# The end of an attention stage reordered: the cap load, two third-chunk sums, the second batch's normalization, and the decoding of one weight unit

## The chip, the core and the metric

The kernel runs on one core of one Trainium2 chip. The metric is the device time of one execution in microseconds (us), lower being better. Engines are called by the profile's names: PE (TensorE matmul) and PEld (TensorE weight load), DVE (VectorE), ACT (ScalarE), POOL (GpSimd), SP (SyncE, which issues most transfers).

## What is computed

Attention with a soft cap over 2 batches, 12 heads, 448 tokens and 64 columns a head, then two feed-forward blocks on the 896 tokens. Cut to what matters here:

```python
scores = cap * tanh((q @ k.T) / sqrt(64) / cap)
attn = softmax(scores)                       # per row
x = (attn @ v) for all heads, as [896 tokens, 768]
h = x @ w_in;  x = (h * sigmoid(1.702 * h)) @ w_out            # d_ff 2048
xn = x / rms(x) * rms_g
out = (silu(xn @ w_gate) * (xn @ w_val)) @ w_out2              # d_ff 1536
```

All inputs and outputs are float32.

## The kernel before, in words

**Attention** (`attention`, lines 174 to 508) works on 12 pairs of heads, p = 0 to 11; pairs 0 to 5 are batch 0, pairs 6 to 11 batch 1. One loop (line 435) runs p from 0 to 12, the last round being only a tail. The order of instructions on every engine is the order of the calls, written by hand. In one round ACT takes tanh and exp of pair p's scores (lines 292 and 295; the first tanh of pair 0 is line 262), TensorE makes the outputs of pair p - 1 (line 314) and the scores of pair p + 1 (line 246), and DVE casts the next q and k (lines 223, 224), copies out pair p - 1 (line 327) and finishes an earlier pair. The scores of each pair come in three chunks of 128 keys and a fourth of 64 keys. `tsc`, the factor of every tanh, is worked out on DVE from the cap (lines 216, 217).

The row sums of exp are made in steps. `add_two` (line 333, DVE) adds chunks one and two into a tile `ts`. `add_third` (line 335) has two meanings: for pair 11 DVE adds the third chunk (line 337); for pairs 1 to 9 (`LAST`, line 329) POOL issues two accumulating transfers that add the fourth chunk. `sums(p)` (line 345) lets TensorE sum over keys by products with ones: one stream for `ts`, one for the third chunk unless it is already in `ts`, and one with `blk` for the fourth chunk unless it is. Each stream is four matmuls, which show as 8 records of line 356. DVE then transposes, takes the reciprocal and transposes again (lines 361, 363, 365). `spread` (line 369) distributes the result by four transfers, for pair 11 two of them from ACT's queue.

`norm(p)` is three steps: `norm_mul` (line 378, DVE) multiplies the output by the reciprocal sums, `norm_hi` writes a rounded copy (line 383 on DVE, line 385 on ACT for pairs 10 and 11), `norm_lo` (line 390, DVE) writes what the rounding left. Both parts go to the feed-forward input x. Round 10 normalizes pairs 4 and 5, round 11 pairs 6 and 7, the tail pairs 8 to 11.

**Feed-forward** (`rest`, from line 510) is a stream of TensorE columns. A column is one block of 128 outputs for one side of the tokens (b = 0: tokens 0 to 383, b = 1: tokens 384 to 895), 18 matmuls (lines 566 to 568, high weight with high x, high weight with low x, low weight with high x, six times). The first ten columns take, as (weight unit i, side b), (0,0), (1,0), (0,1), (1,1), (2,1), (3,1), (2,0), (3,0), (4,0), (5,0). They are called columns 0 to 9 here. b = 1 needs all pairs of batch 1.

**Weights** arrive as 64-bit words and each unit is decoded in six steps: `scale` (line 129, ACT), `shift` (133), `top` (137), `low` (143), all on DVE and all in one tile `dec`; then `high_part` (line 155, ACT) writes the high weights into the ring, and `low_part` (line 160, DVE) the low ones. `low(w)` for w > 2 also starts the load of unit w + 3; units 0 and 1 are decoded in the attention rounds. Unit 2's `scale` runs in round 12 on ACT, its `shift` between the steps of pair 10's normalization, its `top` ahead of pair 11's `norm_mul`, its `low` between pair 11's `norm_hi` and `norm_lo`.

Work that follows a column is put into a list by `at` and carried out in order by `tick` (line 527). Behind column 0 the list is: the rest of pair 11's normalization, then `gate` (line 592, ACT, which needs a new activation table), `high` (line 595, ACT) and `rest_` (line 598, DVE), which waits for `high`; then the list `first` (line 622): scale 3; shift, top, low, high_part, low_part of unit 2 as far as not done; shift, top, low of 3; scale 4; high_part 3, scale 5, shift 4, top 4; then `load_to(5)`. Behind column 1 follow low 4, `rest_` of column 1, and low_part 3.

Of the kernel before, what the change touches and what calls it, by code (L numbers as in the profile page):

```python
# [17 lines left out]
def attn_moe_kernel(  # L18
# [14 lines left out]
    nc = tc.nc  # L33
# [10 lines left out]
    NPR = B * NP  # L44
# [4 lines left out]
    def f(ap):  # L49
        return ap.bitcast(F32)  # L50

    keep = ctx.enter_context(tc.tile_pool(name="keep", bufs=1))
    capt = keep.tile([128, 1], F32, name="capt")
# [108 lines left out]
    def run(op, w):  # L162
        if w < len(units) and (op, w) not in done:
            done.add((op, w))
            op(w)
# [8 lines left out]
    def attention():  # L174
        with ExitStack() as actx:
# [15 lines left out]
            xs, raws, vs, pa, pb, zt, nr, ts_ = {}, {}, {}, {}, {}, {}, {}, {}  # L191
# [15 lines left out]
            cuts = [slice(0, S), slice(64, 192), slice(192, XW - S), slice(0, 64)]  # L207
# [121 lines left out]
            LAST = range(1, NPR - 2)  # L329
# [3 lines left out]
                nc.vector.tensor_tensor(out=ts_[p], in0=pa[p][:, 0], in1=pa[p][:, 1], op=ALU.add)  # L333

            def add_third(p):
                if p == NPR - 1:
                    nc.vector.tensor_tensor(out=ts_[p], in0=ts_[p], in1=pb[p][:, 0:2], op=ALU.add)
                elif p in LAST:
                    for j in range(2):
                        nc.gpsimd.dma_start(  # L340
                            out=ts_[p][half[j], :, j * SH:(j + 1) * SH],
                            in_=pb[p][half[j], 2].rearrange("p (e s) -> p e s", e=2), accum_op=ALU.add,
                        )

            def sums(p):
                ps = ps_s.tile([128, 2, 512], F32, tag="s", name="s")[:, 0]
                streams = [ts_[p], *([] if p == NPR - 1 else [pb[p][:, 0:2]]), *([] if p in LAST else [None])]
                for n, some in enumerate(streams):
                    for e in range(2):
                        for j in range(2):  # L350
                            if some is None:
                                w, t = blk[:, 64 * j:64 * j + 32], pb[p][:, 2, e * SH:(e + 1) * SH]
                            else:
                                w, t = f(ones)[:, 0:32], some[:, e, j * SH:(j + 1) * SH]
                            r0 = 64 * j + 32 * e
                            nc.tensor.matmul(  # L356
                                out=ps[r0:r0 + 32, 0:SH], lhsT=w, rhs=t,
                                start=(n == 0), stop=(n == len(streams) - 1), skip_group_check=True,
                            )
                by_token = zrp.tile([128, SH // 32, 32], F32, tag="bt", name="bt", bufs=2)  # L360
                nc.vector.transpose(out=by_token.rearrange("p b t -> p (b t)"), in_=ps[:, 0:SH])
                few = zrp.tile([128, SH // 32], F32, tag="few", name="few", bufs=2)
                nc.vector.reciprocal(out=few, in_=by_token[:, :, 0])
                nr[p] = zrp.tile([128, SH], F32, tag="rs", name="rs", bufs=2)
                nc.vector.transpose(  # L365
                    out=nr[p], in_=few.rearrange("p (b o) -> p b o", o=1).to_broadcast([128, SH // 32, 32]),
                )
# [9 lines left out]
            def norm_mul(p):  # L377
                nc.vector.tensor_tensor(out=zt[p], in0=zt[p], in1=nr.pop(p), op=ALU.mult)

            def norm_hi(p):  # L380
                b, pp = divmod(p, NP)
                if p < NPR - 2:
                    nc.vector.tensor_copy(xA[0][:, pp, b * S:(b + 1) * S], zt[p])
                else:
                    nc.scalar.activation(out=xA[0][:, pp, b * S:(b + 1) * S], in_=zt[p], func=AF.Copy)

            def norm_lo(p):
                b, pp = divmod(p, NP)
                xx = slice(b * S, (b + 1) * S)
                nc.vector.tensor_tensor(  # L390
                    out=xA[1][:, pp, xx], in0=zt.pop(p), in1=f(xA[0][:, pp, xx]), op=ALU.subtract
                )

            def norm(p):
                for step in (norm_mul, norm_hi, norm_lo):
                    step(p)

            nc.vector.memset(f(xA[0][:, 0, 0:S]), 1.0)
            ts = first_kq()
            nc.scalar.dma_start(out=ts[0], in_=q[0])  # L400
            nc.scalar.dma_start(out=ts[2], in_=k[0, :, cuts[2]])
            nc.scalar.activation(out=tiny, in_=f(ones)[:, 0:1], func=AF.Tanh)
            nc.sync.dma_start(out=ts[1], in_=k[0, :, cuts[1]])
            nc.sync.dma_start(out=capt, in_=cap.rearrange("(o n) -> o n", o=1).to_broadcast([128, 1]))
            nc.sync.dma_start(out=ts[3], in_=k[0, :, cuts[3]])
            constants()
            load_kq(1)
# [22 lines left out]
            scale_by_cap()  # L430

            RAW = {1: 1, 3: 2, 4: 3, 10: 4}
            NORMS = {10: (4, 5), 11: (6, 7), 12: ()}

            for p in range(NPR + 1):
                load_kq(p + 3 if p < 2 else p + 4)
                load_v(p + 2)
                if p == 1:
                    load_kq(5)
                if p in RAW:  # L440
                    load_to(RAW[p])
                if p == 0:
                    first_scores()
                    scores(0, 1)
                    tanh(0, 1)
                    exp(pa[0][:, 0])
                    scores(0, 2)
                    tanh(0, 2)
                    scores_last(0)
                    tanh(0, NC)  # L450
                    exp(pa[0][:, 1])
                    exp(pb[0])
                    outputs(0, (0,))
                    split_kq(1)
                    for c in range(NC):
                        scores(1, c)
                    outputs(0, (1,))
                elif p < NPR:
                    for c in range(NC):
                        tanh(p, c)  # L460
                subtract = cast_kq(p + 2) if p + 2 < NPR else None
                for n in NORMS.get(p, (p - 6,) if p >= 6 else ()):
                    norm(n)
                decode(p, "b")
                if subtract:
                    subtract()
                decode(p, "c")
                if p >= 1:
                    if p == NPR:
                        add_third(p - 1)  # L470
                        sums(p - 2)
                        spread(p - 2)
                    if p < NPR:
                        outputs(p - 1, (NC,))
                        scores_last(p)
                        outputs(p - 1, range(NC) if p > 1 else (2,))
                    else:
                        outputs(p - 1)
                    if p < NPR:
                        copy_out(p - 1, "D")  # L480
                    done_ = p - 1 if p == 1 or p == NPR else p - 2
                    if done_ not in nr:
                        if p == NPR:
                            norm(8)
                        sums(done_)
                        if p == NPR:
                            copy_out(p - 1, "A")
                        spread(done_)
                        if p == NPR:
                            norm(9)  # L490
                if 1 <= p < NPR:
                    tanh(p, NC)
                    exp(pa[p])
                    exp(pb[p])
                if p < NPR:
                    add_two(p)
                    decode(p, "d")
                    if p < NPR - 1:
                        add_third(p)
                if p >= 1:  # L500
                    for c in range(NC):
                        scores(p + 1, c)
            norm_mul(NPR - 2)
            norm_hi(NPR - 2)
            run(shift, 2)
            norm_lo(NPR - 2)
            q_ = NPR - 1
            return lambda: norm_mul(q_), lambda: norm_hi(q_), lambda: run(low, 2), lambda: norm_lo(q_)

    def rest(*norm_last):  # L510
        with ExitStack() as fctx:
# [70 lines left out]
            def later(*fns):  # L582
                at(1, *[("D", True, fn) for fn in fns])
# [27 lines left out]
            for c in range(NC1):  # L611
# [15 lines left out]
                for n, (i, b) in enumerate(order):  # L627
                    last = ()
                    if c == 0 and n == 0:
                        later(lambda: run(top, 2), *norm_last)  # L630
                        last = (
                            lambda: [run(*some) for some in first], lambda: load_to(5), load_g,
                        )
                    ffn1(gA, u0 + i, i, b, slots[n], last)
# [245 lines left out]
```

## Time and profile before

| | us |
|---|---|
| three runs, median | 581.82 |
| three runs, lowest and highest | 581.73, 582.35 |
| the profiled execution, its own time | 581.33 |
| its span, first to last instruction | 579.5 |

| engine | busy us | share of the span |
|---|---|---|
| PE | 573.1 | 99% |
| PEld | 493.4 | 85% |
| DVE | 411.7 | 71% |
| ACT | 274.0 | 47% |
| POOL | 59.1 | 10% |

Times inside the profile count from the span's first instruction. Instructions that follow each other on one engine overlap by their pipelines, so the distance from start to start can be a little under a duration. A releaser named behind an idle time is inferred: it is what ended last before the waiting instruction began.

### The profile page before, as it was taken

What the parts mean: (1) busy time and instruction counts of PE and PEld (TensorE: products, weight loads), DVE (VectorE), ACT (ScalarE), POOL (GpSimd) and SP (SyncE); (2) the same over time, 40 slices, a digit from 0 to 9 for tenths busy, and PEclk for the clock granted to TensorE, in tenths of its full rate; (3) what the DMA queues carried; (4) which work ended last, traced back from release to release, by engine and by line L of the source; (5) the groups of instructions that cost most, each with busy time, mean ns of one, the idle gap of its engine ahead of it and who ended that gap; (6) DMA issues with size and microseconds to landing.
All of it is one profiled execution on the core that took longest, in us unless ns stands there. A gap on an engine that the chain in (4) does not pass through costs nothing.

```text
span 579.5 us, 9374 instructions
## 1 busy us (share of the span) xinstructions
PE 573.1 (99%) x3842; PEld 493.4 (85%) x3842; DVE 411.7 (71%) x568; ACT 274.0 (47%) x369; POOL 59.1 (10%) x54
## 2 busy tenths in 40 slices
PE   8999999999999999999999999999999999999997
PEld 5566668988899998999998989889898998989887
DVE  3889997956653365656787999873787894778732
ACT  7999965755241355553444543442243431334300
POOL 0223300000000000000313013000222000222000
PEclk9999999999999999999999999999999999999999
DMA  8898643642624123233141514351232361232022
GB/s 282 243 225 219 113 116 91 200 146 92 198 67 152 55 81 127 96 123 118 56 156 63 165 59 160 109 164 54 58 110 106 110 217 55 63 108 102 1 92 100
DMA packets 60363, 70.31 MB, mean 121 GB/s; under 512 B 4128, under 2 KB 56480, under 8 KB 60320
## 3 DMA queue, kind: packets, MB, share of 16 engines
q1 hardware_dynamic: 57136, 66.91, 35.5%
q0 software_dynamic: 2592, 2.07, 3.0%
q10 hardware_dynamic: 592, 0.74, 0.4%
q8 instruction: 30, 0.49, 0.3%
q14 instruction: 13, 0.11, 0.1%
HBM read 62.13 MB, written 2.75 MB: 112 GB/s over the span
## 4 chain that ended last, share of the span: by engine, by line
PE 95%; ACT 3%; DMA 1%; issue 0%; DVE 0%; SPq 0%; ACTq 0%
PE b L568 28%; PE b L567 28%; PE b L566 28%; PE v L314 5%; PE s L246 3%; PE s L356 2%; ACT pa L292 1%; PE s L273 1%; ACT pb L292 1%; ACT pb L295 1%; DMA capt<-in_cap 1%; ACT pa L295 1%; ACT pa L262 0%; PE b L705 0%; DVE oacc L775 0%
## 5 line engine op out<-in xcount | busy, mean ns | idle before, releaser
L568 PE MATMUL b<-x,ring 128*128 128x384 f32 (+1 forms) x480 | 174.0, 363 | 0.0
L567 PE MATMUL b<-x,ring 128*128 128x384 f32 (+1 forms) x480 | 173.8, 362 | 0.0
L566 PE MATMUL b<-x,ring 128*128 128x384 f32 (+1 forms) x480 | 173.7, 362 | 0.0
L566 PEld LDWEIGHTS b<-x,ring 128*128 128x128 f32 x480 | 90.1, 188 | 9.8 <-DVE rs L365 0.4
L568 PEld LDWEIGHTS b<-x,ring 128*128 128x128 f32 x480 | 90.1, 188 | 9.6 <-DVE ring L160 0.3
L567 PEld LDWEIGHTS b<-x,ring 128*128 128x128 f32 x480 | 90.1, 188 | 9.6
L160 DVE TENSOR_TENSOR ring<-dec,ring 128x768 fp32r<-128x768 f32 x68 | 77.2, 1136 | 28.1 <-ACT ring L155 28.1
L568 PE MATMUL b<-g,ring 128*128 128x512 f32 (+1 forms) x192 | 69.7, 363 | 0.0
L567 PE MATMUL b<-g,ring 128*128 128x512 f32 (+1 forms) x192 | 69.6, 363 | 0.0
L566 PE MATMUL b<-g,ring 128*128 128x512 f32 (+1 forms) x192 | 69.5, 362 | 0.0
L155 ACT ACTIVATE ring<-dec 128x768 fp32r<-128x768 f32 x66 | 55.2, 837 | 29.8 <-DVE dec L143 24.5
L143 DVE SCALAR_TENSOR_TENSOR dec<-raw,dec 128x768 uint32<-128x768 uint32 x68 | 66.8, 983 | 1.2
L137 DVE SCALAR_TENSOR_TENSOR dec<-raw,dec 128x768 uint32<-128x768 uint32 x68 | 64.8, 953 | 1.0
L129 ACT ACTIVATE dec<-raw 128x768 f32<-128x768 f32 x66 | 59.8, 907 | 5.2 <-issue 2.5
L568 PE MATMUL b<-uA,ring 128*128 128x512 f32 (+1 forms) x144 | 52.1, 362 | 0.0
L567 PE MATMUL b<-uA,ring 128*128 128x512 f32 (+1 forms) x144 | 52.1, 362 | 0.0
L566 PE MATMUL b<-uA,ring 128*128 128x512 f32 (+1 forms) x144 | 52.1, 362 | 0.0
L737 POOL TENSOR_TENSOR a<-a,gg 128x512 f32<-128x512 f32 (+1 forms) x18 | 29.2, 1621 | 187.1 <-DVE gg L730 160.1
L598 DVE TENSOR_TENSOR g<-gg,g 128x384 fp32r<-128x384 f32 (+1 forms) x32 | 20.0, 624 | 39.7 <-ACT g L595 39.7
L740 ACT ACTIVATE uA<-a 128x512 fp32r<-128x512 f32 (+1 forms) x24 | 13.9, 580 | 70.3 <-POOL a L737 52.0
L133 DVE TENSOR_SCALAR dec<-dec 128x768 uint32<-128x768 uint32 x68 | 39.5, 581 | 0.0
L567 PEld LDWEIGHTS b<-g,ring 128*128 128x128 f32 x192 | 36.0, 188 | 3.9
(89 smaller groups left out, 665.5 us busy)
## 6 DMA issues: line engine op xcount, KB each, us to landing
raw<-in_moe_w_out SPq DMA_DIRECT2D x20, 768.0 KB, 4.2
raw<-in_moe_w_in SPq DMA_DIRECT2D x16, 768.0 KB, 4.5
raw<-in_moe_w_gate SPq DMA_DIRECT2D x12, 768.0 KB, 4.2
raw<-in_moe_w_val SPq DMA_DIRECT2D x12, 768.0 KB, 4.3
raw<-in_moe_w_out SPq DMA_DIRECT2D x8, 512.0 KB, 3.6
v<-in_v SPq DMA_DIRECT2D x11, 256.0 KB, 5.1
r<-rs SPq DMA_DIRECT2D x46, 56.0 KB, 3.1
kq<-in_k SPq DMA_DIRECT2D x11, 224.0 KB, 4.9
```

The source lines that it names most:

```text
L129: nc.scalar.activation(out=f(d), in_=f(hi), func=AF.Copy, scale=2.0 ** -112)
L133: nc.vector.tensor_scalar(out=d, in0=d, scalar1=3, scalar2=None, op0=ALU.logical_shift_left)
L137: nc.vector.scalar_tensor_tensor(out=d, in0=hi, scalar=0x80000000, in1=d, op0=ALU.bitwise_and, op1=ALU.bitwise_or)
L143: nc.vector.scalar_tensor_tensor(out=d, in0=lo, scalar=29, in1=d, op0=ALU.logical_shift_right, op1=ALU.bitwise_or)
L155: nc.scalar.activation(out=t[:, 0], in_=f(dec_t[w][0]), func=AF.Copy)
L160: nc.vector.tensor_tensor(out=t[:, 1], in0=f(d), in1=f(t[:, 0]), op=ALU.subtract)
L314: nc.tensor.matmul(out=ps[32 * n:32 * n + 32, j, 0:SH], lhsT=w[:, d0:d0 + 32], rhs=t, start=not before, stop=len(before) == NC, skip_group ...
L566: nc.tensor.matmul(out=wide(o, b), lhsT=w0, rhs=x0, start=first, stop=False)
L567: nc.tensor.matmul(out=wide(o, b), lhsT=w0, rhs=x1, start=False, stop=False)
L568: nc.tensor.matmul(out=wide(o, b), lhsT=w1, rhs=x0, start=False, stop=last)
L598: nc.vector.tensor_tensor(out=gA[1].at(i, hb), in0=gg[0], in1=f(gA[0].at(i, hb)), op=ALU.subtract)
L737: eng.tensor_tensor(out=t[0], in0=t[0], in1=t[1], op=ALU.mult)
```

## The change

Four things are changed.

1. The cap is loaded first on SP's queue, ahead of the first chunk of k; the second piece of that pair's k (`ts[2]`, on ACT's queue) keeps its place in its queue.
2. For pairs 9 and 10 DVE adds the third chunk into `ts`, as for pair 11, so `sums(9)` and `sums(10)` have one stream less. Pair 9 keeps its accumulating transfers, now behind that addition.
3. Round 10 normalizes only pair 4, round 11 only pair 5. Pairs 6 and 7 are normalized in the tail around `sums(11)`; behind them come the steps of pairs 8, 9 and 10, interleaved, with `norm_hi` of 8 and 9 on ACT too; then pair 11.
4. `shift`, `top` and `low` of unit 2 are no longer called between those steps. They run from the list `first`, so behind column 0's `rest_`.

```diff
-                if p == NPR - 1:
+                if p >= NPR - 3:
                     nc.vector.tensor_tensor(out=ts_[p], in0=ts_[p], in1=pb[p][:, 0:2], op=ALU.add)
-                elif p in LAST:
+                if p in LAST:
...
-                streams = [ts_[p], *([] if p == NPR - 1 else [pb[p][:, 0:2]]), *([] if p in LAST else [None])]
+                streams = [ts_[p], *([] if p >= NPR - 3 else [pb[p][:, 0:2]]), *([] if p in LAST else [None])]
...
-                if p < NPR - 2:
+                if p < NPR - 4:
                     nc.vector.tensor_copy(xA[0][:, pp, b * S:(b + 1) * S], zt[p])
...
             nc.scalar.dma_start(out=ts[0], in_=q[0])
+            nc.sync.dma_start(out=capt, in_=cap.rearrange("(o n) -> o n", o=1).to_broadcast([128, 1]))
+            nc.sync.dma_start(out=ts[1], in_=k[0, :, cuts[1]])
             nc.scalar.dma_start(out=ts[2], in_=k[0, :, cuts[2]])
             nc.scalar.activation(out=tiny, in_=f(ones)[:, 0:1], func=AF.Tanh)
-            nc.sync.dma_start(out=ts[1], in_=k[0, :, cuts[1]])
-            nc.sync.dma_start(out=capt, in_=cap.rearrange("(o n) -> o n", o=1).to_broadcast([128, 1]))
...
-            NORMS = {10: (4, 5), 11: (6, 7), 12: ()}
+            NORMS = {10: (4,), 11: (5,), 12: ()}
...
                         if p == NPR:
-                            norm(8)
+                            norm(6)
                         sums(done_)
                         if p == NPR:
                             copy_out(p - 1, "A")
                         spread(done_)
                         if p == NPR:
-                            norm(9)
+                            norm(7)
+                            for step, n in (
+                                (norm_mul, 8), (norm_hi, 8), (norm_mul, 9), (norm_hi, 9), (norm_lo, 8),
+                                (norm_mul, 10), (norm_hi, 10), (norm_lo, 9), (norm_lo, 10),
+                            ):
+                                step(n)
...
-            norm_mul(NPR - 2)
-            norm_hi(NPR - 2)
-            run(shift, 2)
-            norm_lo(NPR - 2)
             q_ = NPR - 1
-            return lambda: norm_mul(q_), lambda: norm_hi(q_), lambda: run(low, 2), lambda: norm_lo(q_)
+            return lambda: norm_mul(q_), lambda: norm_hi(q_), lambda: norm_lo(q_)
...
-                        later(lambda: run(top, 2), *norm_last)
+                        later(*norm_last)
```

## Rows read from the trace of the kernel before

**Rows 1.** The page, busy time, share of the span and instructions of each engine.

```profile
PE 573.1 (99%) x3842; PEld 493.4 (85%) x3842; DVE 411.7 (71%) x568; ACT 274.0 (47%) x369; POOL 59.1 (10%) x54
```

**Rows 2.** The chain that ended last, in order of time: start us, us, what.

```profile
0.76 0.38 SPq L403
1.19 3.89 DMA capt<-in_cap
5.56 1.16 ACT pa L262 x2
...
78.33 1.89 PE s L356 x40
```

**Rows 3.** Windows: stretch, length, busy time of each engine, granted clock, DMA share, GB/s.

```profile
140.00:300.00 160.00, 160.00 (x799) 144.17 (x799) 95.01 (x123) 69.60 (x107) 5.96 (x5) 1.00 0.34 109
```

**Rows 4.** Timeline of PE: start us, us, engine, line, operation, tiles, shapes, count.

```profile
78.53 0.56 PE L356 MATMUL s<-pb,ones 128*32 128x224 f32 x8
...
98.41 0.39 PE L566 MATMUL b<-x,ring 128*128 128x512 f32 x1
...
102.71 0.39 PE L567 MATMUL b<-x,ring 128*128 128x512 f32 x1
103.00 0.50 PE L568 MATMUL b<-x,ring 128*128 128x512 f32 x1
```

**Rows 5.** Waits from 98 to 110 us: who waited for whom, total, times, longest.

```profile
PEld b L568 <- DVE ring L160: 0.3, 1, 0.3
```

**Rows 6.** Timeline of DVE, from the tail to unit 3.

```profile
81.33 1.09 DVE L337 TENSOR_TENSOR ts<-ts,pb 128x896 f32<-128x896 f32 x1
...
87.55 0.62 DVE L378 TENSOR_TENSOR z<-z,r 128x448 f32<-128x448 f32 x1
88.08 0.55 DVE L133 TENSOR_SCALAR dec<-dec 128x768 uint32<-128x768 uint32 x1
88.81 0.63 DVE L390 TENSOR_TENSOR x<-z,x 128x448 fp32r<-128x448 f32 x1 [0.18 <-ACT x L385]
89.36 0.95 DVE L137 SCALAR_TENSOR_TENSOR dec<-raw,dec 128x768 uint32<-128x768 uint32 x1
90.22 0.62 DVE L378 TENSOR_TENSOR z<-z,r 128x448 f32<-128x448 f32 x1
...
93.91 0.56 DVE L598 TENSOR_TENSOR g<-gg,g 128x384 fp32r<-128x384 f32 x1 [1.67 <-ACT g L595]
95.45 0.96 DVE L160 TENSOR_TENSOR ring<-dec,ring 128x768 fp32r<-128x768 f32 x1 [0.97 <-ACT ring L155]
96.32 0.55 DVE L133 TENSOR_SCALAR dec<-dec 128x768 uint32<-128x768 uint32 x1
...
97.90 0.96 DVE L143 SCALAR_TENSOR_TENSOR dec<-raw,dec 128x768 uint32<-128x768 uint32 x1
...
102.00 0.95 DVE L160 TENSOR_TENSOR ring<-dec,ring 128x768 fp32r<-128x768 f32 x1
```

**Rows 7.** Timeline of ACT, behind column 0.

```profile
91.54 1.28 ACT L592 ACT_TABLE_LOAD   x1
...
94.58 0.83 ACT L155 ACTIVATE ring<-dec 128x768 fp32r<-128x768 f32 x1
```

**Rows 8.** DMA issues from 91 to 98.5 us: count, size, us from issue to landing.

```profile
raw<-in_moe_w_in SPq DMA_DIRECT2D x1, 768.0 KB, 4.5
```

**Rows 9.** Timeline of PE at the start: first scores of pair 0.

```profile
4.08 1.12 PE L256 MATMUL s<-first,first 64*128 64x224 f32 x4
...
5.74 0.95 PE L246 MATMUL s<-first,first 64*128 64x448 f32 x4
```

**Rows 10.** DMA issues of the first 6 us, the first chunk of k on SP's queue.

```profile
first<-in_k SPq DMA_DIRECT2D x1, 64.0 KB, 2.6
```

**Rows 11.** Timeline of PE at the start: the last two warm-up products.

```profile
3.20 0.95 PE L417 MATMUL s<-x,ones 128*128 128x448 f32 x2
3.57 0.58 PE L417 MATMUL s<-x,ones 128*128 128x448 f32 x1
```

## The prediction, made before the changed kernel ran

> **What bounds the kernel now.** First the busy times: TensorE works for 99% of the span [rows 1], so only what shortens its work, or makes it wait, can move the time much. Next the chain of waits: it begins with the cap's transfer (1.19 to 5.08 us) and ScalarE's first tanh at 5.56, and late in the attention it lies on TensorE's sums [rows 2]. Then the stretches of the feed-forward part: between 140 and 300 us TensorE is busy in all 160.00 us [rows 3]. There is no gap later that could swallow a delay: a microsecond lost at 100 us is lost at the end. Last the timelines around the hand-over. In TensorE's there is one hitch: in column 5 the first product with unit 3's low weights starts at 103.00, 0.29 after the product before it [rows 4], where 19 products from 98.41 to 102.71 lie 0.226 apart. The waits name the cause: VectorE's low_part [rows 5], which ran from 102.00 to 102.95 [rows 6]. So before the change unit 3's decoding on VectorE is already just in time, with nothing in hand. That is what the reader should keep in view.
>
> **Part 1, shorter sums.** Two third-chunk streams go, of 8 records each; the next eight records start 0.38 later (78.53 to 78.91, as the stream of pair 10 does), so TensorE is done 0.76 sooner [rows 4]. VectorE pays two additions of 1.09 [rows 6], in rounds 9 and 10. The cover is that rounds 10 and 11 each lose one normalization, at least two instructions of 0.6; without that cover TensorE's outputs would wait for the copy-out behind them. Pair 9's two POOL transfers now wait for VectorE's addition; behind them on POOL's queue is nothing of the attention, and their sum is read only at 78 us, some 8 us later. Cost nothing.
>
> **Part 2, the tail of the normalization.** From the addition for pair 11 to pair 11's multiplication (81.33 to 90.22 [rows 6]) the list on VectorE changes as follows. Gone are shift 2 (88.08 to 88.81, 0.73 with a wait of 0.18) and top 2 (89.36 to 90.22, 0.86): 1.59. New are four steps, two multiplications and two subtractions, at 0.53 from start to start (87.55 to 88.08): 2.12. The rounded copies of pairs 8 and 10 are made on ScalarE with a subtraction waiting behind each: I put 0.18 for each, as in the row at 88.81: 0.36. The start of all this is earlier by up to 0.38, because sums(9) ends that much sooner and VectorE was waiting on it; I take 0.38. Sum: 2.12 + 0.36 - 1.59 - 0.38 = 0.51 later. Bounds: 0 if the copies are quite hidden and a step is shorter, 1.2 if nothing is gained at the start and each wait doubles.
>
> Pair 11's multiplication then starts at 90.73. For pair 10 the subtraction ended 1.89 after the multiplication's start (87.55 to 88.81 + 0.63), so pair 11's low half is there at 92.62. TensorE wants it in column 2's seventeenth product, 20 products ahead of 98.41: at 93.89 before, at 93.13 with the shorter sums. Half a microsecond in hand: no wait there. Pairs 6 to 10 are earlier still, and the reciprocals of pair 11, spread by ACT's and SP's queues, leave no later than before. All six outputs and reciprocals of the batch now live together, but the normalizations of pairs 4, 5 and 6 free each buffer ahead of its next use.
>
> **Part 3, unit 2's decoding, which decides.** Before, VectorE's wait for ScalarE (rounded copy of pair 11, table load of 1.28 [rows 7], gate, high) was partly filled with low 2, and shift and top had gone before. Now all three stand behind `rest_`, which waits for ScalarE. From pair 11's multiplication to `rest_` it was 93.91 - 90.22 = 3.69, all of it paced by ScalarE, which has no less to do; so `rest_` comes 0.51 later, at 94.42. From `rest_` to low_part 2 it was 95.45 - 93.91 = 1.54 [rows 6]. Now it is 0.47 for `rest_` (0.56, less the 0.09 by which VectorE's instructions overlap at 95.45 and 96.32), 1.58 for shift and top (96.32 to 97.90, unit 3's), 0.96 for low, 0.04 to ScalarE, 0.83 for high_part [rows 7], 0.04 back: 3.92. That is 2.38 more, or 2.89 with part 2. So low_part 2 starts at 98.34, and ends at 99.30.
>
> TensorE would be in column 4 at 98.41 - 0.76 = 97.65. It waits there some 0.65 for the high weights and 0.55 for the low ones. From low_part 2 to low_part 3 VectorE takes 6.55 (95.45 to 102.00 [rows 6]) in one unbroken string that includes column 1's `rest_`; so low_part 3 runs from 104.89, and the product that started at 103.00 starts at 105.89, after a wait of about 2.4. From there both engines are late by the same 2.89, and TensorE never catches up [rows 3]. The 0.76 of part 1 is eaten by these waits.
>
> One queue hangs on this: unit 5's load on SP waits for low 2, which ended near 91.7 (90.22 + 0.53 + 0.96) and now ends at 97.43. It lands 4.5 later [rows 8], at 101.9; ScalarE takes it behind unit 3's high_part, at 97.90 + 0.96 + 0.04 + 0.83 + 2.89 = 102.62. It is covered by 0.7; beyond that each microsecond of delay would be paid in full, since column 1's `rest_` and low_part 3 stand behind it.
>
> **Part 4, the cap first.** The tanh factor was ready at 5.5. The first scores (four records) start at 4.08 and end at 5.20; those of the next chunk end at 5.74 + 0.95 = 6.69 [rows 9], and ScalarE, done with two tanh at 6.72 [rows 2], takes them at once. So an earlier cap lets the first two tanh begin, but the third must still wait for TensorE: a gain of 0.05 at most. Against it, the first k chunk is issued 0.43 later (1.19 for 0.76). It landed at 0.76 + 2.6 = 3.36 [rows 10], and its use at 4.08 leaves 0.72. If it takes over the cap's 3.89 with its place [rows 2], it lands at 5.08 and all is 1.0 later. With 2.6 from 1.19 it lands at 3.79. The second is the nearer row, since it is the same transfer; some delay behind the cap's 128 small packets is likely, and I put a loss of 0.10. By the Trainium skill, DMA: Bandwidth & Descriptors, Queues, rings and completion order, a transfer's completion is reported only after the same engine's earlier writes; that would tie the chunk to the end of the cap's writes and speaks for the larger loss, 585.7 in all. No row shows the chunk behind the cap.
>
> **Sum.** 2.89 + 0.10 = 2.99 on the profiled execution's 581.33 (span 579.5): 584.3. That execution lies 0.49 under the median of 581.82, so the forecast is **584.8**. The case's own ends are 2.38 - 0.05 (part 2 at 0) and 3.58 + 1.00 above the median: 584.2 to 586.4.
>
> **Rivals.** (a) The decoding is not the bound and TensorE keeps part 1: faster. The place is unit 3's low_part: it would have to start near 101.0 instead of 104.89, that is, the three steps of unit 2 must find room ahead of `rest_`. Then 0.76, the hitch of 0.06 and 0.05 for the cap are saved: 580.9. For it: VectorE idles 1.67 there. Against it: VectorE takes its list in order, and the list puts them behind.
>
> (b) TensorE's clock falls in the waits. The last warm-up products, 448 columns, start 0.37 apart [rows 11], 0.83 ns a column, where 512 columns later take 0.226, 0.44 ns: two speeds a factor of two apart, though the granted clock's row says 1.00 of the later stretch [rows 3]. If the wait of 2.4 costs the higher level for one column's 18 products, that is 18 x 512 x 0.39 ns = 3.6 more: 588.4. Against it: the waits are broken up by products. The Trainium skill, TensorE: Matmul & The Clock Gate, Part 1, has idle time put the engine to 1.2 GHz and work bring back 2.4; by that rule a wait this long may or may not do it, and no row of this trace has a wait of the kind.
>
> (c) The delay is absorbed: 581.8, if TensorE had waits later on that shrink. The stretch from 140 to 300 has none.
>
> **Chances.** Forecast 0.84; (a) 0.07; (b) 0.06; (c) 0.03. A change under 0.2% (1.2 us) can't be told from none. Faster 0.07, same 0.03, slower 0.90. The range takes the case's own ends with a little below, where the copies and the start of the tail are better than put: 583.9 to 586.4. It leaves out (a), (b) and (c), 0.16 in all.
>
> **What would show it.** On VectorE after the change: shift, top and low of unit 2 behind the first L598, low_part 2 near 98.3 and low_part 3 near 104.9. On TensorE: waits for the ring in columns 4 and 5, about 1.2 and 2.4, and all later columns 2.9 late. The sums of pairs 9 and 10 with one stream less, column 0 some 0.7 sooner. The first tanh before 5.56 but the third not before 6.7. I am wrong if columns 4 and 5 start without a wait, or if TensorE waits in column 2 for pair 11, or if unit 5's load, not VectorE, ends the wait.

## The result, and the profile after

| | before | changed |
|---|---|---|
| median, us | 581.73 | 588.07 |
| lowest and highest of five, us | 580.99, 582.35 | 586.34, 588.12 |
| span of the profiled execution, us | 579.5 | 584.6 |

The changed kernel is slower: ratio 1.0104, 95% interval 1.0091 to 1.0117. The forecast of 584.8, with a range up to 586.4, had the sign and the main place of the loss, but only 3.0 of the 6.3 us. The profiled execution took 586.34; it is the fastest of the five. The other four had spans of 586.0 to 586.3 and a mean granted clock of 0.997 where this one has 1.000, and that difference is one of the two things that had to be found out. One run of a later kernel, the profiled one of the cap alone, took 818.52 at a granted clock of 0.658; it is left out, so that experiment has times but no profile to read.

The page's busy times, against [rows 1]: TensorE has 16 instructions less, as meant, but is busy for a smaller share.

```profile
PE 574.5 (98%) x3826; PEld 493.6 (84%) x3826; DVE 413.6 (71%) x568; ACT 275.1 (47%) x371; POOL 59.0 (10%) x54
```

The chain that ended last (start us, us, what), against [rows 2]. It began with the cap's transfer; now it begins with the first piece of k, and with TensorE's first scores.

```profile
1.19 3.96 DMA first<-in_k
5.29 1.86 PE s L256 x8
7.15 1.51 PE s L246 x4
...
97.63 0.97 DVE dec L137
98.62 0.97 DVE dec L143
99.62 0.85 ACT ring L155
100.49 0.96 DVE ring L160
```

Its lower half is the decoding of unit 2, none of which was on the chain before. The transfers of the first 6 us (size, us from issue to landing), against [rows 10] and these further rows of the kernel before:

```profile
first<-in_q ACTq DMA_DIRECT2D x1, 224.0 KB, 2.9
first<-in_k ACTq DMA_DIRECT2D x1, 128.0 KB, 4.3
...
first<-in_k SPq DMA_DIRECT2D x1, 32.0 KB, 4.0
```

In the changed kernel:

```profile
first<-in_q ACTq DMA_DIRECT2D x1, 224.0 KB, 4.2
...
first<-in_k SPq DMA_DIRECT2D x1, 64.0 KB, 4.0
...
capt<-in_cap SPq DMA_DIRECT2D x1, 0.5 KB, 3.7
```

The cap was issued 0.44 sooner and was used at 4.44 in place of 5.11. But q, on the other queue and issued at the same time (0.75), took 4.2, and the piece of k, now second, 4.0 in place of 2.6. TensorE and ScalarE at the start, against [rows 9] and these two rows of the kernel before:

```profile
5.74 1.70 PE L246 MATMUL s<-first,first 64*128 64x448 f32 x8
```

```profile
6.73 1.01 ACT L292 ACTIVATE pa<-s,tsc 128x896 f32<-128x896 f32 x1
```

In the changed kernel:

```profile
5.29 1.86 PE L256 MATMUL s<-first,first 64*128 64x224 f32 x8 [1.13 <-DMA first<-in_k]
6.91 3.22 PE L246 MATMUL s<-first,first 64*128 64x448 f32 x8
```

```profile
6.44 1.38 ACT L262 ACTIVATE pa<-s,tsc 128x448 f32<-128x448 f32 x2 [3.26 <-PE s L256]
8.68 1.01 ACT L292 ACTIVATE pa<-s,tsc 128x896 f32<-128x896 f32 x1 [0.86 <-PE s L246]
```

The third tanh, at 6.73 before, starts at 8.68: 1.95 later. Of this 1.21 is the wait for the transfers (4.08 to 5.29), and 0.74 lies between the first scores and the third tanh, 3.39 in place of 2.65: the eight products of line 246 span 3.22 in place of the 1.70 that they took before.

VectorE at the hand-over, against [rows 6]; 1.95 is to be taken off each time to compare. Between the second and the third row lie shift, top and low of unit 2, from 97.04 on.

```profile
92.88 0.62 DVE L378 TENSOR_TENSOR z<-z,r 128x448 f32<-128x448 f32 x1
...
96.57 0.56 DVE L599 TENSOR_TENSOR g<-gg,g 128x384 fp32r<-128x384 f32 x1 [1.73 <-ACT g L596]
...
100.49 0.96 DVE L160 TENSOR_TENSOR ring<-dec,ring 128x768 fp32r<-128x768 f32 x1 [0.91 <-ACT ring L155]
...
107.02 0.95 DVE L160 TENSOR_TENSOR ring<-dec,ring 128x768 fp32r<-128x768 f32 x1
```

And TensorE: the start of column 0, in the kernel before and in the changed one, then columns 4 and 5 of the changed kernel, against [rows 4]:

```profile
83.86 0.44 PE L566 MATMUL b<-x,ring 128*128 128x384 f32 x1
```

```profile
85.09 0.45 PE L567 MATMUL b<-x,ring 128*128 128x384 f32 x1
...
100.51 0.50 PE L567 MATMUL b<-x,ring 128*128 128x512 f32 x1 [0.68 <-ACT ring L155]
...
101.51 0.50 PE L569 MATMUL b<-x,ring 128*128 128x512 f32 x1 [0.26 <-DVE ring L160]
...
108.02 0.50 PE L569 MATMUL b<-x,ring 128*128 128x512 f32 x1 [2.14 <-DVE ring L160]
```

Three waits, 3.1 in all, for the high part of unit 2, its low part, and the low part of unit 3. The last product started at 103.00 before, so TensorE is 5.02 late here: 1.95 from the start and 3.07 from the hand-over. The span grew by 5.1. Nothing is lost or won behind this point.

### The profile page after: what moved, and what is told of

Its sections match the earlier page's. It is cut to its first block, busy times and chain, and to the rows that moved or that the text cites. A ratio compares the mean times of both kernels' runs of the same rounds, so it can differ in the third digit from the quotient of the medians.

```text
span 584.6 us, 9346 instructions
## 1 busy us (share of the span) xinstructions
PE 574.5 (98%) x3826; PEld 493.6 (84%) x3826; DVE 413.6 (71%) x568; ACT 275.1 (47%) x371; POOL 59.0 (10%) x54
## 4 chain that ended last, share of the span: by engine, by line
PE 91%; ACT 4%; DVE 3%; DMA 1%; issue 1%; SPq 0%; DVEq 0%; ACTq 0%
PE b L569 27%; PE b L568 27%; PE b L567 27%; PE v L314 5%; PE s L246 3%; PE s L356 1%; PE s L273 1%; ACT pb L295 1%; DMA first<-in_k 1%; ACT pa L295 1%; ACT pa L292 1%; ACT pb L292 0%; DMA r<-rs 0%; DVE dec L143 0%; DVE dec L137 0%
```

## The experiments

The first four undo or apply one part each. All were run against the kernel before on the same chip; its median there was 581.53.

**The cap alone.** The kernel before with this part only (here and below the cap's broadcast is cut to `cap...`):

```diff
+            nc.sync.dma_start(out=capt, in_=cap...)
+            nc.sync.dma_start(out=ts[1], in_=k[0, :, cuts[1]])
             nc.scalar.dma_start(out=ts[2], in_=k[0, :, cuts[2]])
...
-            nc.sync.dma_start(out=ts[1], in_=k[0, :, cuts[1]])
-            nc.sync.dma_start(out=capt, in_=cap...)
```

> The kernel before with the cap first on SP's queue and nothing else changed. Theory A (the start's loss is the cap's packets holding up q and the first piece of k, and is passed on in full): first scores near 5.3, third tanh near 8.7 instead of 6.73, span about 579.5 + 1.96 = 581.5, time 583.3. Rival B (the start's delay is absorbed later in the attention): span 579.5, time 581.7. On the clock: if the granted clock of 0.997 that four of five runs of the changed kernel showed comes from the start, most runs here show it too and take about 585.0; if it comes from TensorE's waits in columns 4 and 5, all runs here show 1.0.

Median 583.42, ratio 1.0029 (1.0017 to 1.0040); the spans of its six runs were 581.5 to 581.7, each at a granted clock of 1.000. Theory A holds in its time and span to 0.2, B falls: the start's loss is passed on whole. The start itself, first scores and third tanh, is not read here; the changed kernel above and two kernels below show it. And the cap alone does not bring the 0.997.

**All but the cap.**

```diff
-            nc.sync.dma_start(out=capt, in_=cap...)
-            nc.sync.dma_start(out=ts[1], in_=k[0, :, cuts[1]])
...
+            nc.sync.dma_start(out=ts[1], in_=k[0, :, cuts[1]])
+            nc.sync.dma_start(out=capt, in_=cap...)
             nc.sync.dma_start(out=ts[3], in_=k[0, :, cuts[3]])
```

> The changed kernel with the cap put back to its old place. Theory A: span 584.6 - 1.96 = 582.6, third tanh at 6.73, low_part 3 near 105.05. On the clock: if the 0.997 comes from the waits in columns 4 and 5, most runs show it and take 584.4 + 1.7 = 586.1; if it comes from the start, all runs are at 1.0 and 584.4. Rival: cap and decoding overlap, and undoing the cap gains less than 1.

Median 584.53, ratio 1.0055 (1.0042 to 1.0067): 3.0 over the kernel before, where the forecast had 2.9 for parts 1 to 3. Three of five runs had a span of 582.7, as theory A said. The profiled one had 583.6, because its third tanh started at 7.77, though nothing at the start differs from the kernel before. Only one run showed 0.997, so neither half of the sentence on the clock came true; the waits are the same as in the changed kernel:

```profile
107.08 0.50 PE L569 MATMUL b<-x,ring 128*128 128x512 f32 x1 [2.16 <-DVE ring L160]
```

**All but the cap and the decoding's place.** On top of the last edit:

```diff
-                                (norm_mul, 10), (norm_hi, 10), (norm_lo, 9), (norm_lo, 10),
+                                (norm_mul, 10), (norm_hi, 10), (norm_lo, 9),
                             ):
                                 step(n)
+                            run(shift, 2)
+                            norm_lo(10)
...
-            return lambda: norm_mul(q_), lambda: norm_hi(q_), lambda: norm_lo(q_)
+            return lambda: norm_mul(q_), lambda: norm_hi(q_), lambda: run(low, 2), lambda: norm_lo(q_)
...
-                        later(*norm_last)
+                        later(lambda: run(top, 2), *norm_last)
```

> The changed kernel with the cap put back and with shift, top and low of unit 2 called where the kernel before calls them, between the steps of pairs 10 and 11; sums and normalizations as changed. Theory C (two causes: the moved normalizations lengthen VectorE's list ahead of rest_ as well as the moved decoding): low_part 3 near 103.8, span about 579.5 + 1.8 = 581.3, time 583.1. Rival D (only the place of the three decoding steps costs, the rest gains the 0.76 of the shorter sums): span 578.8, time 580.6.

Median 583.64, ratio 1.0035 (1.0023 to 1.0047), profiled span 581.2. VectorE, then TensorE's waits, of this kernel:

```profile
103.63 0.95 DVE L160 TENSOR_TENSOR ring<-dec,ring 128x768 fp32r<-128x768 f32 x1
```

```profile
93.23 0.49 PE L569 MATMUL b<-x,ring 128*128 128x512 f32 x1 [0.29 <-ACT x L385]
93.97 0.50 PE L570 MATMUL b<-x,ring 128*128 128x512 f32 x1 [0.24 <-DVE x L390]
104.64 0.50 PE L571 MATMUL b<-x,ring 128*128 128x512 f32 x1 [1.29 <-DVE ring L160]
```

Its third tanh started at 6.55, 0.18 before that of the kernel before, so low_part 3 is 103.63 + 0.18 - 102.00 = 1.81 late: theory C, 1.8. Rival D falls. With the decoding back in its place, the moved normalizations push it off by that much (the shorter sums, still in this kernel, let VectorE's tail start 0.23 sooner and cannot be the reason), and now pair 11's halves are late for column 2 as well (the two short waits near 93 and 94).

**The decoding's place alone.**

```diff
-            run(shift, 2)
...
-            return lambda: norm_mul(q_), lambda: norm_hi(q_), lambda: run(low, 2), lambda: norm_lo(q_)
+            return lambda: norm_mul(q_), lambda: norm_hi(q_), lambda: norm_lo(q_)
...
-                        later(lambda: run(top, 2), *norm_last)
+                        later(*norm_last)
```

> The kernel before with only shift, top and low of unit 2 moved behind rest_; cap, sums and normalizations as before. Pair 11's multiplication can start 1.59 sooner on VectorE, but not ahead of its reciprocals, near 89.0, so rest_ comes some 1.2 sooner and low_part 3 2.38 - 1.2 = 1.2 later: span 580.7, time 582.5 (theory C). Rival D: the place of the three steps is the whole loss: low_part 3 some 2.9 later, span 582.4, time 584.2. On the clock: a wait of about 1 us in column 5 should leave it at 1.0 if only longer waits lower it.

Median 583.50, ratio 1.0032 (1.0019 to 1.0045).

```profile
89.46 0.63 DVE L390 TENSOR_TENSOR x<-z,x 128x448 fp32r<-128x448 f32 x1 [0.65 <-ACT x L385]
90.01 0.62 DVE L378 TENSOR_TENSOR z<-z,r 128x448 f32<-128x448 f32 x1
...
104.16 0.95 DVE L160 TENSOR_TENSOR ring<-dec,ring 128x768 fp32r<-128x768 f32 x1
```

The third tanh of this profile started at 7.39, 0.66 late. Against the start, pair 11's multiplication is at 89.35 and low_part 3 is 104.16 - 0.66 - 102.00 = 1.50 late: nearer to C (1.2) than to D (2.9), but 0.3 over it. As C said, the three steps cost 2.38 less what VectorE gains ahead of them; the gain is 0.87 (90.22 to 89.35) of the 1.59 that was taken off its list. Pair 10's subtraction, which shift 2 used to hide, now waits 0.65 in place of 0.18 for the rounded copy on ScalarE, and so the multiplication behind it does not get down to 89.0. The time alone, 2.0 over the kernel before, lies between the forecasts of 582.5 and 584.2 and does not decide. Behind the moved normalizations the same three steps cost less, 3.07 - 1.81 = 1.26, so the two causes do not simply add. TensorE's wait in column 5 was 1.29 in the last kernel and 1.39 in this one, and the clock stayed at 0.999 or 1.000 in all eleven runs of the two.

The next four are about the start and the clock.

**The changed kernel again**, unchanged, for a profile of an execution like the four.

> The changed kernel as it is, for a profile at the granted clock of 0.997 that four of its five runs showed. Theory F (TensorE's wait of about 2.1 in column 5 lowers the clock): a stretch behind 105 us shows a granted clock of 0.5, its products start about twice as far apart as 0.227, the waits there stay as they are, and the span is near 586.3. Rival G (the clock falls at the start): the low stretch lies before 12 us and the third tanh is later than 8.7. In a profile at 1.0 the span is near 584.6 and nothing is told apart.

Median 587.95, ratio 1.0106 (1.0092 to 1.0120); three of four at 0.997, the profiled one among them, with a span of 586.2. Its stretches (length, busy time of PE, PEld, DVE, ACT, POOL, then the granted clock, the DMA share and GB/s):

```profile
106.00:108.00 2.00, 0.00 (x0) 0.00 (x0) 1.81 (x4) 1.94 (x5) 0.00 (x0) 1.00 1.07 339
108.00:110.00 2.00, 1.87 (x5) 1.50 (x6) 2.00 (x4) 1.97 (x4) 0.00 (x0) 0.54 1.09 325
110.00:112.00 2.00, 2.00 (x7) 1.63 (x6) 1.97 (x4) 1.97 (x4) 0.00 (x0) 0.60 0.22 74
112.00:114.00 2.00, 2.00 (x11) 1.72 (x10) 2.00 (x4) 1.65 (x3) 0.00 (x0) 1.00 0.85 279
```

And its TensorE products there:

```profile
108.13 0.79 PE L569 MATMUL b<-x,ring 128*128 128x512 f32 x1 [2.16 <-DVE ring L160]
108.71 0.63 PE L567 MATMUL b<-x,ring 128*128 128x512 f32 x1
109.14 0.63 PE L568 MATMUL b<-x,ring 128*128 128x512 f32 x1
...
111.66 0.40 PE L568 MATMUL b<-x,ring 128*128 128x512 f32 x1
```

Theory F holds. TensorE stood still for 2.16, and afterwards the granted clock is 0.54, then 0.60 over two stretches that hold both of the engine's levels: the lower, 1.2 GHz, until about 111.4, then 2.4 GHz again. At the lower the products start 0.43 apart (109.14 less 108.71), at the higher 0.227. From 108.13 to 111.66 there are eight distances, 3.53 in all; at 0.227 they would take 1.82, and in the profile of 584.6 the eight behind the same wait took 1.95 (108.02 to 109.97). So the lower level cost 1.6 to 1.7, and the span is 586.2 - 584.6 = 1.6 longer. Here the third tanh started at 8.78, so G falls. In the profile of 584.6 the same wait, 2.14, left the clock at 1.00. So the wait can lower the clock and need not. Without the cap's part it did so in at most one run of five (the one at 0.997 above); what decides was not found.

**The first piece of k on ACT's queue.**

```diff
             nc.scalar.dma_start(out=ts[0], in_=q[0])
+            nc.sync.dma_start(out=capt, in_=cap...)
+            nc.scalar.dma_start(out=ts[1], in_=k[0, :, cuts[1]])
             nc.scalar.dma_start(out=ts[2], in_=k[0, :, cuts[2]])
...
-            nc.sync.dma_start(out=ts[1], in_=k[0, :, cuts[1]])
-            nc.sync.dma_start(out=capt, in_=cap...)
```

> The kernel before with the cap first on SP's queue and the first piece of k moved to ACT's queue, behind q and ahead of the second piece. Theory P (the cap's 128 tiny packets hold up all that is in flight on the shared DMA engines, whatever its queue): q lands near 4.9 and the piece near 5.1 again, first scores near 5.3, third tanh near 8.7, span 581.5. Rival R (only what stands behind the cap in its own queue waits): q lands near 3.7, the piece near 3.9, first scores at 4.08, third tanh between 6.6 and 7.8 as in the kernel before, span 579.5 to 580.5.

Median 583.21, ratio 1.0029 (1.0017 to 1.0041), span 581.6.

```profile
first<-in_q ACTq DMA_DIRECT2D x1, 224.0 KB, 4.1
...
first<-in_k ACTq DMA_DIRECT2D x1, 64.0 KB, 4.1
...
capt<-in_cap SPq DMA_DIRECT2D x1, 0.5 KB, 3.7
```

Nothing stands in ACT's queue ahead of q, and only q ahead of the piece of k, and yet both are as late as behind the cap. First scores at 5.40, third tanh at 8.79. Theory P holds in its main point: the cap's 512 bytes hold up what is in flight for another queue. Rival R falls. Why they do so is not shown by this.

**The piece of k in second place, behind other keys.**

```diff
+            nc.sync.dma_start(out=ts[3], in_=k[0, :, cuts[3]])
             nc.sync.dma_start(out=ts[1], in_=k[0, :, cuts[1]])
             nc.sync.dma_start(out=capt, in_=cap...)
-            nc.sync.dma_start(out=ts[3], in_=k[0, :, cuts[3]])
```

> The kernel before with the first piece of k second on SP's queue behind the 32 KB of its last keys, and the cap third. Theory P: packets of 256 bytes hold up nothing, the piece lands near 1.19 + 2.7 = 3.9, first scores at 4.08; the cap lands near 5.5 in place of 5.08, so the first tanh starts near 6.0 and the third near 7.2. Rival R' (the second place in the queue is what costs, whatever stands ahead): the piece lands near 5.1 and the first scores start near 5.3.

```profile
first<-in_q ACTq DMA_DIRECT2D x1, 224.0 KB, 2.7
first<-in_k ACTq DMA_DIRECT2D x1, 128.0 KB, 2.9
first<-in_k SPq DMA_DIRECT2D x1, 64.0 KB, 2.5
first<-in_k SPq DMA_DIRECT2D x1, 32.0 KB, 2.2
capt<-in_cap SPq DMA_DIRECT2D x1, 0.5 KB, 4.1
```

Second place costs the piece nothing: 2.5 from its issue. The second piece of k on ACT's queue even lands after 2.9, where it took 4.3 with the cap ahead of it in time. First scores at 4.08; the cap, last, lets the first tanh start only at 6.18 and the third at 7.23, as expected. Median 582.32, ratio 1.0016 (1.0007 to 1.0025). So it is the cap's transfer, not the place. Nor is it the number of rows: the 32 KB ahead of the piece of k are 256 bytes to each of 128 partitions, the cap 4 bytes to each of 128. The cap differs in two ways, its rows are tiny and all of them read the same 4 bytes of memory; no run separates these.

**Nine warm-up products behind the cap.** On top of the cap's part alone:

```diff
-    WARM = 6
+    WARM = 9
```

> The kernel before with the cap first and nine warm-up products in place of six, so that TensorE is busy until about 5.2, when the late q and k arrive. Theory H (0.75 of the cap's loss comes from TensorE working at half speed behind its idle 1.13): the first scores still start near 5.3, but the products of the second chunk start 0.19 apart in place of 0.37, the third tanh starts near 7.9 in place of 8.7, span 580.8. Rival I (the half speed has nothing to do with the gap): third tanh near 8.7, span 581.6.

Median 582.11, ratio to the kernel before 1.0011 (1.0002 to 1.0019): 1.3 of the cap's 1.9 are back.

```profile
5.33 1.03 PE L256 MATMUL s<-first,first 64*128 64x224 f32 x8 [0.21 <-DMA first<-in_k]
6.17 1.70 PE L246 MATMUL s<-first,first 64*128 64x448 f32 x8
```

The data come as late as before (5.33), but with TensorE busy until then the eight products of line 256 span 1.03 in place of 1.86, those of line 246 1.70 in place of 3.22, and the third tanh starts at 7.15, sooner than theory H had it. This is one profile, and below a start without a gap is as late as 7.77; but the spans of all eleven runs here, 580.0 to 580.9, lie under the six of the cap alone, 581.5 to 581.7. Rival I falls. The granted clock's row reads 1.00 through the first 10 us of all these profiles; the distances between products are what tells the two speeds apart here.

The last three look for a version that beats the kernel before. **The table loaded early**: the cap and decoding as before, the shorter sums, pair 7 alone moved to the tail, the rounded copies of pairs 8 and 9 on ScalarE with the steps interleaved, and this (cut to the added table load):

```diff
...
-                            norm(8)
+                            nc.scalar.activation(out=tiny, in_=f(ones)[:, 0:1], func=AF.Silu)
+                            norm(7)
                         sums(done_)
...
```

> A version of the kernel before with the cap and the decoding in their old places, with the shorter sums of pairs 9 and 10, pair 7 alone moved into the tail, the rounded copies of pairs 8 and 9 on ScalarE, and a one-column Silu put ahead of the tail's copy-out so that the activation table is loaded while ScalarE has nothing to do. If the table load is on the path to rest_ as the traces say: pair 11's multiplication near 90.5, rest_ near 93.0 in place of 93.91, low_part 3 near 101.1 in place of 102.0, no wait for the ring in columns 4 and 5, and TensorE keeps the 0.76 of the shorter sums: span some 0.8 under the kernel before, 578.9, time 580.7. Rival (ScalarE is not what paces rest_, or VectorE's two additions delay a copy-out that TensorE waits for): span 579.7 or more, time 581.5 or more.

```profile
91.56 0.62 DVE L378 TENSOR_TENSOR z<-z,r 128x448 f32<-128x448 f32 x1
...
93.82 0.56 DVE L601 TENSOR_TENSOR g<-gg,g 128x384 fp32r<-128x384 f32 x1 [0.24 <-ACT g L598]
```

From pair 11's multiplication to `rest_` it is now 2.26 in place of 3.69, so ScalarE's table load did pace it. But the multiplication itself is late, because VectorE waited 1.04 for ScalarE, which was issuing two transfers (1.40 of its time) ahead of pair 8's copy. Median 581.44, ratio 0.9998 (0.9989 to 1.0007): the 580.7 that was expected did not come. **That wait filled** with shift and top of unit 2:

```diff
-                                (norm_mul, 8), (norm_hi, 8), (norm_mul, 9), (norm_hi, 9), (norm_lo, 8),
-                                (norm_mul, 10), (norm_hi, 10), (norm_lo, 9),
+                                (norm_mul, 8), (norm_hi, 8), (norm_mul, 9), (norm_hi, 9), (lambda w: run(shift, w), 2),
+                                (lambda w: run(top, w), 2), (norm_lo, 8), (norm_mul, 10), (norm_hi, 10), (norm_lo, 9),
...
-            run(shift, 2)
...
-                        later(lambda: run(top, 2), *norm_last)
+                        later(*norm_last)
```

> The version with the early table load, where VectorE waited 1.04 for ScalarE (which was issuing transfers) ahead of pair 8's subtraction; shift and top of unit 2 are put into that wait. Theory: the 1.34 of these two steps leave the list behind it and all but 0.3 of them is hidden, so pair 11's multiplication and low_part 3 come about 1.0 sooner against the start; no wait for the ring in column 5, TensorE keeps most of the 0.76 of the shorter sums: span 579.0 at the middle of the starts, median 580.8, ratio to the kernel before 0.9988. Rival (the start's variation of up to 1 and another wait behind it, pair 11's low half or a PSUM bank, take it back): median 581.4.

TensorE has no wait left in columns 2 to 5, but one of 0.21 in the attention, at 75.23, which the last version has and the kernel before has not, stays. Median 581.44, ratio 0.9994 (0.9985 to 1.0003): not told apart from the kernel before, and the 580.8 that was expected did not come. The profiled execution's third tanh started at 7.48, 0.75 later than in the profile of before, with a span only 0.3 longer. So some 0.45 of the 0.76 may be won, which the start's own variation hides. **Eight warm-up products** in the kernel before were to narrow that:

```diff
-    WARM = 6
+    WARM = 8
```

> The kernel before with eight warm-up products in place of six. In the traces at hand the third tanh starts anywhere from 6.55 to 7.77 with the same start of the kernel, according to when TensorE's products go from 0.37 to 0.19 apart. Theory H' (a longer stretch of full-width products brings the higher speed earlier and more surely): first scores near 4.85, third tanh at 6.5 to 6.8 in every run, times closer together than 580.9 to 582.9 and a median near 581.2. Rival (the two more products only put the first scores off by 0.75): third tanh 0.2 to 0.7 later, time 581.8 to 582.2.

Median 581.41, ratio 1.0000 (0.9991 to 1.0009), runs from 581.03 to 582.53: no narrower, a miss. In its profile the third tanh started at 7.77, though TensorE had no gap ahead of its first scores. No version here is shown to be faster than the kernel before.

## Why the prediction was right and wrong

**Part 1, shorter sums: right.** Column 0 starts at 85.09; less the 1.95 of the start that is 0.72 sooner than the 83.86 of before, where 0.7 was forecast. The waits of columns 4 and 5 eat it, as was said.

**Part 2, the tail: 0.71 in place of 0.51.** Pair 11's multiplication is at 92.88 - 1.95 = 90.93. The earlier start that I put at 0.38 was 81.33 - (83.05 - 1.95) = 0.23. TensorE did not wait for pair 11 in column 2.

**Part 3, the decoding: right.** `rest_` came 3.69 behind the multiplication, the same as before. From it to low_part 2 took 3.92, as worked out; from there to low_part 3 6.53, with 6.55 forecast. Low_part 3, less the start, is 3.07 late for a forecast 2.89, and the kernel without the cap's part came out 3.0 over the kernel before. Unit 5's load did not end a wait: its `scale` followed the high part of unit 3 at once.

**Part 4, the cap: the step that failed.** "The second is the nearer row, since it is the same transfer", I wrote of the piece of k, and put 0.10, with 1.00 as the far end. It cost 1.95. Nor did the first tanh come before 5.56, which was to show it; it started at 6.44.

With 1.95 in place of 0.10 the sum gives 586.65; the two executions that kept the clock took 586.34 and 586.47, at the end of the range, and the other seven need the clock as well.

Three errors made the difference. I looked at the transfer that changed its place and not at q, which kept its own; q's landing went from 2.9 to 4.2 although nothing in its queue was altered. I wrote that no row shows the chunk behind the cap, but the trace of before has two other pieces of k, issued with it and behind it: the 32 KB right behind it on SP's queue took 4.0, where 64 KB ahead of it took 2.6, and the 128 KB on ACT's queue took 4.3. In that trace q and the first piece of k, both issued at 0.76 and ahead of the cap (1.19), landed at 3.66 and 3.36, the two others at 5.66 and 5.51, behind the cap's 5.08. With the cap issued behind them, in the experiment on the second place, the 32 KB took 2.2 and the 128 KB 2.9. And I let the loss be as long as the transfers' delay, when TensorE, idle for 1.13 while it waited, then worked at half speed for longer: 0.74 more. With three more warm-up products the third tanh came 1.53 sooner than in the changed kernel, which is that 0.74 and as much again.

The Trainium skill, DMA: Bandwidth & Descriptors, Queues, rings and completion order, says that a transfer's completion lands only after earlier writes of the same DMA engine, across its queues. The later q and piece of k agree with that, in that the 512 bytes of the cap, issued no later than q, took 3.7; but whether it is that order or the time that the cap's rows take that holds q up, no run here separates.

**Rival (b), the clock: the second step that failed.** The sum had nothing for it; as a rival it was given 0.06 and 588.4, one column's eighteen products at the lower level. In four of the five runs it came, in seven of nine counting the second set of runs, on top of the forecast and not in its place, and cost 1.6 to 1.7: seven or eight products rather than eighteen. My reason against it, that the waits are broken up by products, was no reason: the wait of 2.16 is in one piece. That the median, 588.07, is near the rival's 588.4 is luck: the rival had 0.10 for the cap and 3.6 for the clock. The Trainium skill, TensorE: Matmul & The Clock Gate, Part 1, has idle time lower the clock to 1.2 GHz and work raise it to 2.4; the 0.54 and 0.60 behind the wait agree, and the 1.00 behind the same wait in the other profile shows that the length of the wait alone does not settle it.

The sum, as it stands now: 3.07 for the hand-over, 1.95 for the start, 1.7 for the clock in most executions; on the 581.33 of the profiled execution that is 588.05. Rivals (a) and (c) did not come.

## What to carry to other kernels

When the order of two small loads is changed, look at every transfer that is in flight then, on all queues, and price a load by a row of the same transfer, or of one beside it, and not by its bytes: here 512 bytes took 3.7 and 32 KB took 2.2. A wait that is added to TensorE can have two prices, its length and a lower clock behind it; the new wait of 2.1 brought 1.6 to 1.7 more in seven of nine executions, and such a price belongs into the forecast with its chance. And an engine that decodes "just in time" has no room for three more instructions behind a wait, however idle it looks: count its list from the last thing that paces it.

## What was not expected of the hardware

- A load of 4 bytes to each of 128 partitions took 3.5 to 4.3 as first, second or third of its queue, and when it was issued first, at 0.75, 224 KB on another queue landed after 4.1 to 4.3 in place of 2.7 to 3.0.
- With the same instructions at the start, the third tanh began anywhere from 6.45 to 7.77 in the profiles, by when TensorE's products went from the wider distance to the narrower. The kernel before itself spreads from 580.8 to 582.9 over its runs. The start can account for as much, but the starts of the unprofiled runs are not known.
- The activation table's load took 1.28 and the next function started right behind it, at 95.49 behind 94.19 + 1.28; issuing two transfers held ScalarE for 1.2 to 1.4.
